# One hand-listed order replaced by another in an attention and gated-convolution kernel, with all eight weight units' low words merged on VectorE

## Chip, cores, metric

The kernel runs on one core of a Trainium2 chip. The metric is the device time of one execution in microseconds; a kernel's time is the median of several runs.

## What is computed

For 8 batches, 8 heads, 576 tokens and a head size of 64, the reference computes softmax attention inside chunks of 64 tokens, and then a gated layer on the joined heads (width 512), all in float32:

```python
scores = scale * np.matmul(q_c, k_c.transpose(0, 1, 2, 4, 3))      # chunks of 64
attn = np.exp(scores - max) ; attn = attn / (sum + 1e-9)
x = attn @ v_c                                                     # tokens x 512
gate = sigmoid(sum over k of conv_w[k] * x[s - 4 + k])             # 5 taps, causal
out = (gate * (x @ w_val)) @ w_out
```

## The kernel before

The 4608 tokens are worked on in nine groups of 512 (0 to 8). Each group has two pairs of 128 rows of the width (p = 0, 1); a pair's tile holds two halves (b = 0, 1). The last group, 8, collects the last 64 tokens of every batch and needs the last four columns of the groups before it.

Both big products are made from split operands: each operand is a high word rounded to TensorE's fp32r format and a low word with what is left, and three products (high x high, low x high, high x low) are added. The weights arrive as 64-bit numbers and are split on the chip too. A weight matrix (v for w_val, o for w_out) is split in four units, 0 to 3.

The order of all the work is written out by hand. The string `ORDER` (lines 19 to 82) lists pieces; the loop at the end of the kernel calls them one by one, and each engine runs its instructions in that order (`run`, line 136, records every instruction, so all carry line 137 in the profile). A list of slots, `SLOTS` (lines 85 to 95), says which buffer each new tile takes: SBUF tiles z, PSUM banks b, and two buffers for exponentials, e. A piece that reuses a buffer waits for its last reader.

The pieces that the text speaks of, with their arguments (g group, p pair, n weight matrix, c unit or quarter of the width):

- `lw`, `lq`, `lk`, `lv` (lines 164 to 195): loads on SP's queue; a third number loads one half, 256 KB, else 512 KB.
- `w1` to `w9`, `wa`, `wb` (lines 218 to 285): the splitting of a weight unit. `w1` clamps, `w2` scales, `w3` takes the sign, `w4` joins the bits, `w6` rounds the high word. The low 32 bits come in either by `w5` (line 249, a ScalarE multiply) and `w8` (line 258, a multiply on GpSimd, or on VectorE as `w8D`), or by `w58` (line 262, one VectorE instruction for both). Then `wa` subtracts and `wb` adds (GpSimd, or VectorE as `waD`, `wbD`), or, for units 1 to 3 of v, TensorE sums three terms (`Q`, line 273) and ScalarE copies them out (`wc`).
- `S` (line 287): scores, 32 small matmuls per half. `mx` maxima, then one of three ways to the exponential: `sb` and `ex` (lines 333, 336: VectorE subtracts the maximum, ScalarE takes the exponential of the whole tile); `mh`, `M`, `exM` (lines 342 to 359: the maximum is split in two words, eight matmuls in all subtract it in PSUM, and ScalarE reads the exponential from there); or `ng` and `ea` (lines 366, 370: ScalarE takes it row by row, with the maximum as the bias, and sums along). `sm` or `rc`: sums and reciprocals.
- `nm` (line 393; `nmD` on VectorE): normalization. `T` transposes, `ec` copies them out, `A` the weighted sums of v. `xr`, `xd` (lines 439, 444): high and low word of x; `xc`: x itself, for the taps.
- `k0`, `k`, `kx`, `kk` (lines 487 to 535): first tap and the others, kx and kk for two groups at once. `sg` sigmoid.
- `V` (line 548): product of x with w_val, three matmuls, or one of the three if a fourth number is given. `vc` copies it out, `gs` multiplies by the gate, `gr` and `gd` make high and low word.
- `P` (line 574): product with w_out, three matmuls. `oc`, `o1` copy out, `st`, `s1` store. `W` (line 603): matmuls on zeros ahead of the first data.

A letter behind a name moves the piece: D to VectorE, G to GpSimd.

Of the kernel before, what the change touches and what calls it, by code (L numbers as in the profile page):

```python
# [31 lines left out]
vc 0 1,lk 2 0,S 2 0 0,lv 1 1,S 2 0 1,mx 2 0,V 0 0 3 0,V 0 1 0 1,V 0 0 1 2,lv 3 1,sb 2 0,V 0 1 3 0,lv 2 1,k 0 2 2,w3 o 2,nm 1 1,
xc 1 0,w5 o 2,T 1 1,ec 1 1,V 1 0 0,w1G o 0,V 1 0 1,k 0 1 3,ex 2 0,sm 2 0,vc 0 0,w1G o 1,A 1 1,xr 1 1,xd 1 1,k0 1 1,w2 o 2,
w5 o 0,lk 2 1,S 2 1 0,S 2 1 1,mx 2 1,V 1 2 0,V 1 3 0,V 1 3 1,ng 2 1,V 1 1 3,k 0 2 4,xc 1 1,w4 o 2,V 1 1 0,V 1 1 2,V 1 0 2,
lq 7 1,V 1 2 2,k 0 0 3,k 0 3 4,hc 0 1,lq 4 0,w2 o 0,nm 2 0,T 2 0,V 1 2 1,k 0 2 3,k 0 0 2,w3 o 1,k 0 0 4,k0D 1 0,lk 4 0,V 1 1 1,
# [4 lines left out]
ea 3 1,nm 3 0,wa o 3,V 2 0 1,sb 4 0,wbD o 0,wbD o 3,V 2 2 1,rc 3 1,V 2 0 3,w6 o 2,gr 0 1,V 2 3 2,T 3 0,ec 3 0,lv 5 1,vc 2 1,  # L40
lq 4 1,lk 5 1,gr 0 0,V 2 0 2,V 2 1 3,vc 2 0,S 4 1 0,waD o 2,A 3 0,xc 3 0,ex 4 0,S 4 1 1,lq 8 0,nmD 3 1,gdD 0 1,P 0 2 3,P 0 3 3,
k 1 0 4,lv 8 0,wbD o 2,P 0 3 2,gdD 0 0,w4 o 1,w7 o 1,w6 o 1,w8 o 1,wa o 1,T 3 1,ec 3 1,lk 7 1,mx 4 1,P 0 2 0,xr 3 0,hc 1 0,
k0 1 2,k0 2 3,lk 6 0,P 0 3 0,P 0 2 2,P 0 0 2,sb 4 1,sm 4 0,A 3 1,P 0 0 3,wb o 1,lv 6 0,ex 4 1,hc 1 1,xd 3 0,hc 2 0,sm 4 1,
P 0 3 1,xr 3 1,xc 3 1,lq 5 1,xd 3 1,P 0 2 1,S 5 1 1,S 5 1 0,P 0 1 0,oc 0 1,mx 5 1,ng 5 1,V 3 1 0,k 1 1 2,k0 2 0,k 2 0 4,V 3 1 2,
k 1 2 1,k0 2 2,k 1 1 1,k 2 2 4,lk 6 1,nm 4 0,k 1 2 3,k 1 1 3,k0 1 3,k 2 3 2,k 1 3 1,ea 5 1,k 1 2 2,k0 2 1,P 0 1 1,V 3 1 1,T 4 0,
ec 4 0,V 3 0 0,k 1 3 3,k 1 1 4,k 1 0 2,sg 1 0,k 1 2 4,P 0 0 0,V 3 0 3,V 3 1 3,k 1 3 4,nm 4 1,T 4 1,ec 4 1,P 0 0 1,k 2 1 4,
lv 4 1,rc 5 1,V 3 2 3,V 3 3 2,k 1 3 2,k 2 1 2,V 3 3 3,V 3 3 1,V 3 3 0,lv 4 0,gs 1 0,sg 1 1,gs 1 1,gr 1 0,lq 5 0,V 3 0 1,P 0 1 3,
k 2 1 1,V 3 2 1,lk 8 0,k 2 0 2,V 3 0 2,vc 3 0,P 0 1 2,oc 0 0,V 3 2 2,V 3 2 0,gr 1 1,A 4 0,S 5 0 0,vc 3 1,k 2 3 1,S 5 0 1,xr 4 0,
gdD 1 0,P 1 3 0,P 1 2 0,xc 4 0,hc 4 0,lk 7 0,gdD 1 1,P 1 0 2,P 1 1 3,k 2 2 3,P 1 2 3,mx 5 0,xd 4 0,P 1 1 0,sb 5 0,ex 5 0,
k 2 1 3,P 1 2 1,lq 7 0,nm 5 1,T 5 1,lq 8 1,P 1 2 2,k 2 0 3,k 2 2 1,k 2 3 4,P 1 3 2,lq 6 0,P 1 3 3,k 2 0 1,k0 4 0,k 2 2 2,  # L50
P 1 3 1,k 2 3 3,P 1 0 1,sg 2 0,gs 2 0,sg 2 1,P 1 1 1,gs 2 1,ec 5 1,gr 2 0,P 1 0 0,P 1 1 2,P 1 0 3,oc 1 1,oc 1 0,S 6 0 1,gd 2 0,
lv 5 0,S 6 1 0,S 6 1 1,S 6 0 0,A 4 1,sm 5 0,nm 5 0,P 2 1 1,gr 2 1,gd 2 1,P 2 1 0,P 2 0 1,lk 8 1,P 2 0 0,mx 6 1,mx 6 0,sb 6 0,
sb 6 1,S 7 0 1,ex 6 0,sm 6 0,nm 6 0,S 7 0 0,A 5 1,xc 4 1,mx 7 0,P 2 1 3,P 2 1 2,P 2 0 3,xr 4 1,xd 4 1,lv 7 0,P 2 0 2,st 0 1,
P 2 2 2,xr 5 1,ex 6 1,sm 6 1,xd 5 1,xcD 5 1,kx 4 2,P 2 3 1,st 1 1,sb 7 0,ex 7 0,P 2 3 3,kk 4 2 3,P 2 2 1,oc 2 0,st 0 0,P 2 2 0,
T 5 0,ec 5 0,P 2 3 0,P 2 3 2,P 2 2 3,oc 2 1,sm 7 0,hc 2 1,S 7 1 1,S 7 1 0,nm 6 1,S 8 0 0,S 8 0 1,T 6 0,ec 6 0,hc 0 0,V 4 0 2,
hc 5 1,V 4 0 0,nm 7 0,mx 7 1,sb 7 1,mx 8 0,ex 7 1,T 6 1,ec 6 1,sb 8 0,ex 8 0,V 4 0 3,A 5 0,xc 5 0,lv 6 1,A 6 1,xc 6 1,S 8 1 1,
sm 7 1,nm 7 1,sm 8 0,xr 5 0,S 8 1 0,mx 8 1,V 4 1 0,V 4 0 1,xd 5 0,hc 6 1,V 4 1 3,xr 6 1,xd 6 1,sb 8 1,V 4 1 2,k0D 4 1,T 7 1,
V 4 1 1,vc 4 0,k0D 5 0,lv 8 1,T 7 0,kk 4 2 4,nm 8 0,V 4 2 2,k 4 1 3,st 1 0,ec 7 1,st 2 0,ec 7 0,kk 4 2 2,T 8 0,ec 8 0,hc 4 1,
ex 8 1,V 4 2 1,k 5 0 1,V 4 3 3,A 6 0,xc 6 0,A 7 0,xr 6 0,kk 4 2 1,sm 8 1,xd 6 0,xc 7 0,xr 7 0,A 8 0,V 4 3 1,xr 8 0,V 4 3 2,
# [641 lines left out]
```

## Time and profile before

| | us |
|---|---|
| median of 3 runs (lowest, highest) | 286.02 (285.7, 286.69) |
| the profiled execution, device time | 287.65 |
| its span, first to last instruction | 285.9 |
| TensorE matmuls busy | 273.0 |
| VectorE busy | 245.3 |
| ScalarE busy | 192.1 |
| GpSimd busy | 56.6 |

PE is TensorE (PEld its weight loads), DVE VectorE, ACT ScalarE, POOL GpSimd, SP the engine whose queue issues the loads and stores. In the names of tiles z and ys are SBUF buffers, b PSUM banks, e_row exponentials, mx maxima, rs sums. In a row of instructions the arrow points from what is read to what is written; "x64" is a count. Square brackets at a row's end hold how long the engine had been idle and whose work released it; "issue" means that the profile shows nothing it waited for. Stage and break are told by TensorE's idle time, since that engine is the busiest.

### The profile page before, as it was taken

Reading aid. Unit: us, or ns where it says so; the run is one execution under the profiler, and the core shown is the slowest. Engines: PE = TensorE matmul, PEld = TensorE weight load, DVE = VectorE, ACT = ScalarE, POOL = GpSimd, SP = SyncE. Lnnn points to the kernel's source line nnn. Section 1 sums busy time; section 2 is a strip of 40 time slices with the busy share of each in tenths; the row PEclk is TensorE's granted clock in tenths of the full one; section 3 lists DMA queues with packets and bytes.
Section 4 is the critical chain, followed back from the end, with each engine's and each line's share of the span. In section 5 each row is a group of like instructions: output and inputs, shape, how many; then the busy total and the mean of one; then the engine's idle time right before and its main releaser. Section 6 shows DMA issues by size and latency. Waiting matters only on the chain.

```text
span 285.9 us, 7884 instructions
## 1 busy us (share of the span) xinstructions
PE 273.0 (96%) x3378; PEld 219.5 (77%) x3378; DVE 245.3 (86%) x322; ACT 192.1 (67%) x345; POOL 56.6 (20%) x58
## 2 busy tenths in 40 slices
...
GB/s 212 389 408 407 404 406 409 314 230 149 220 6 14 135 221 202 97 270 255 70 150 2 5 0 5 0 0 2 0 0 1 2 0 40 34 76 147 147 302 212
DMA packets 14754, 42.46 MB, mean 149 GB/s; under 512 B 1536, under 2 KB 1792, under 8 KB 14720
## 3 DMA queue, kind: packets, MB, share of 16 engines
...
## 4 chain that ended last, share of the span: by engine, by line
PE 88%; DVE 4%; DMA 3%; issue 2%; SPq 1%; ACT 1%; DVEq 0%
PE b L137 88%; DVE z L137 3%; DMA z<-in_q 3%; SPq L137 1%; ACT z L137 1%; DVE mx L137 0%; DVE e_row L137 0%; DVEq L137 0%
## 5 line engine op out<-in xcount | busy, mean ns | idle before, releaser
L137 PE MATMUL b<-z,v_hi 128*128 128x512 f32 x288 | 96.4, 403 | 1.5 <-DVE z L137 1.4
L137 PE MATMUL b<-o_hi,z 128*128 128x512 f32 (+1 forms) x296 | 94.7, 392 | 0.0
L137 ACT COPY z<-b 128x1024 f32<-128x1024 f32 (+2 forms) x65 | 61.0, 963 | 42.4 <-PE b L137 37.5
L137 PEld LDWEIGHTS b<-z,v_hi 128*128 128x128 f32 x288 | 53.7, 188 | 16.4 <-DVE mx L137 1.9
L137 PEld LDWEIGHTS b<-o_hi,z 128*128 128x128 f32 x296 | 55.2, 188 | 12.7
L137 PE MATMUL b<-z,v_lo 128*128 128x512 f32 x144 | 56.3, 397 | 1.7 <-issue 1.7
L137 PE MATMUL b<-o_lo,z 128*128 128x512 f32 (+1 forms) x148 | 57.5, 389 | 0.0
L137 DVE SCALAR_TENSOR_TENSOR z<-z,cw,z 128x508 f32<-128x508 f32 (+3 forms) x80 | 55.8, 742 | 0.1
L137 POOL TENSOR_TENSOR z<-e_row,rs 128x1024 f32<-128x1024 f32 (+1 forms) x15 | 28.0, 1866 | 63.9 <-ACT z L137 24.7
L137 ACT ACTIVATE z<-z 128x1024 f32<-128x1024 f32 (+3 forms) x27 | 22.3, 837 | 17.6 <-DVE z L137 17.6
L137 DVE TENSOR_TENSOR z<-z,z 128x1024 f32<-128x1024 f32 (+3 forms) x25 | 30.7, 1244 | 2.3 <-ACT z L137 2.2
L137 PEld LDWEIGHTS b<-o_lo,z 128*128 128x128 f32 x148 | 28.0, 189 | 5.8
L137 DVE SCALAR_TENSOR_TENSOR ys<-ys,cw 128x1018 f32<-128x1018 f32 (+7 forms) x32 | 31.1, 1008 | 0.9 <-ACT ys L137 0.7
L137 PEld LDWEIGHTS b<-z,v_lo 128*128 128x128 f32 x144 | 27.1, 188 | 5.5
L137 PEld LDWEIGHTS b<-z,z 64*64 64x64 f32 x1088 | 19.3, 143 | 8.8 <-issue 5.4
L137 PE MATMUL b<-z,z 64*64 64x64 f32 x1088 | 21.6, 230 | 4.5 <-issue 3.5
L137 DVE TENSOR_REDUCE mx<-b 128x16 f32<-128x1024 f32 (+1 forms) x19 | 22.0, 1164 | 4.4 <-PE b L137 4.2
L137 DVE TENSOR_TENSOR z<-b,z 128x1024 fp32r<-128x1024 f32 (+1 forms) x19 | 21.9, 1156 | 3.1 <-ACT z L137 2.4
L137 ACT CAST z<-b 128x1024 fp32r<-128x1024 f32 (+1 forms) x19 | 18.4, 985 | 5.3 <-PE b L137 3.8
L137 ACT ACTIVATE e_row<-b,mx 128x64 f32<-128x64 f32 x72 | 21.4, 359 | 0.4 <-DVE mx L137 0.4
L137 ACT ACTIVATION_READ_ACCUMULATOR e_row<-b,mx 128x1 f32 x72 | 18.0, 252 | 0.0
L137 DVE TENSOR_REDUCE rs<-e_row 128x16 f32<-128x1040 f32 (+1 forms) x14 | 16.6, 1183 | 0.7 <-ACT e_row L137 0.7
...
## 6 DMA issues: line engine op xcount, KB each, us to landing
...
```

What stands on the lines that cost most here:

```text
L137: return tc.keep_in_program_order(fn(*args, **kwargs))
```

## The change

`ORDER` and `SLOTS` are replaced as a whole; no function is changed. What is computed stays the same. The new list has 1024 pieces in place of 1033:

- all eight units (v 0 to 3, o 0 to 3) use `w58`; before, v 3 alone. The seven `w5` on ScalarE, the `w8D` of v 0, 1, 2 and the `w8` of o 0 to 3 are gone;
- `wb` of o 0, 2, 3 and `wa` of o 2 go from VectorE to GpSimd;
- pair (0, 1) takes the exponential row by row in both halves (before: the first half), pair (0, 0) by `sb` and `ex` (before: `M`); `M` is not used any more;
- `k0` is on VectorE 4 times in place of 9, `kx` once in place of twice; `nm` on VectorE 4 times in place of 2; `xc` 5 1 and `o1` 8 3 go to ScalarE;
- the first loads come as v 3, taps, v 1, k, q (first half of pair (0, 1)), v 2; before, v 2 came ahead of k and q. v 0 comes ahead of group 1's q;
- every later piece has another place; TensorE's products, loads and stores are the same in number and size.

```diff
-ORDER = """lw v 3,zw,W 3,w1 v 3,w2 v 3,lc,w1 c 0,w2 c 0,zi,zs 0,W 9 22,w3 c 0,lw v 1,w3 v 3,w4 v 3,w6 v 3,zs 1,lw v 2,w7 v 3,lk 0 1 0,
-lq 0 1 0,w1 v 1,w2 v 1,lk 0 1 1,w3 v 1,w58 v 3,w4 v 1,zr 1,w3 v 2,lq 0 0 0,lq 0 1 1,Q v 3,w4 c 0,w7 c 0,w7 v 1,S 0 1 0,w5 v 1,
-lk 0 0 1,w5 c 0,w8D c 0,lk 0 0 0,w5 v 2,w1 v 2,w8D v 1,w6 v 1,Q v 1,mx 0 1 0,ng 0 1 0,lq 0 0 1,S 0 1 1,w2 v 2,w4 v 2,w7 v 2,
-wc v 3,w9,ea 0 1 0,S 0 0 0,w8D v 2,S 0 0 1,w6D v 2,Q v 2,wc v 2,mx 0 1 1,wc v 1,mh 0 1 1,M 0 1 1,exM 0 1 1,mx 0 0,mh 0 0,M 0 0,
-exM 0 0,zr 0,rc 0 1 0,nmD 0 1 0,T 0 1 0,ec 0 1 0,lq 1 0,lw v 0,w1 v 0,lk 1 0,S 1 0 1,w2 v 0,w3 v 0,sm 0 1 1,S 1 0 0,lv 0 1,
-A 0 1 0,xr 0 1 0,nm 0 1 1,T 0 1 1,V 0 3 2 0,V 0 2 2 0,xc 0 1 0,lw o 3,V 0 2 2 1,ec 0 1 1,k0 0 2,V 0 3 2 1,A 0 1 1,sm 0 0,w5 v 0,
-mx 1 0,xd 0 1 0,nm 0 0,sb 1 0,xc 0 1 1,xr 0 1 1,w3 o 3,T 0 0,w4 v 0,ec 0 0,V 0 3 2 2,V 0 0 2 1,V 0 1 2 1,lq 1 1,ex 1 0,
-V 0 0 2 0,V 0 3 3 0,V 0 3 3 1,w1G o 3,lv 0 0,A 0 0,w6 v 0,xr 0 0,V 0 1 3 1,w7 v 0,w8D v 0,wa v 0,lv 1 0,xd 0 1 1,V 0 1 3 2,
-V 0 2 3 2,V 0 0 3 2,sm 1 0,xc 0 0,lk 1 1,S 1 1 1,S 1 1 0,V 0 0 3 1,V 0 0 1 0,k0 0 3,V 0 2 1 1,V 0 2 0 1,nm 1 0,xd 0 0,V 0 2 1 0,
-V 0 2 3 1,V 0 0 0 2,w2 o 3,mx 1 1,lq 2 0,lw o 2,T 1 0,V 0 0 0 0,w5 o 3,wbD v 0,V 0 2 1 2,k0 0 0,lw o 1,w5 o 1,V 0 2 3 0,
...
-S 3 1 0,xc 2 0,w7 o 0,k 1 0 1,gs 0 0,gs 0 1,w8 o 0,A 2 1,xr 2 1,xd 2 1,w8 o 2,S 3 1 1,mx 3 1,V 2 3 1,k 1 0 3,ex 3 0,xc 2 1,
...
-o1D 8 3,s1 8 3,P 8 1 1,o1 8 2,P 8 1 2,P 8 1 3,o1 8 1,P 8 0 2 0,s1 8 1,P 8 0 3 0,s1 8 2,P 8 0 1 0,P 8 0 0 0,P 8 0 1 1,P 8 0 3 1,
-o1 8 0 0,s1 8 0 0,P 8 0 0 1,o1 8 0 1,s1 8 0 1"""
...
+ORDER = """zi,zw,lw v 3,w3 v 3,W 9 22,zs 1,w1 v 3,W 3,lc,w1 c 0,w5 c 0,w3 c 0,w2D v 3,lw v 1,w4 v 3,w7 v 3,w2 c 0,w3 v 1,lk 0 1 0,zs 0,
+w1 v 1,lq 0 1 0,lw v 2,lk 0 1 1,lq 0 1 1,w6 v 3,w4 c 0,w58 v 3,Q v 3,lq 0 0 0,lk 0 0 0,w2 v 1,w4 v 1,w6 v 1,w7 v 1,S 0 1 0,
+w58 v 1,Q v 1,w1 v 2,mx 0 1 0,w7 c 0,wc v 3,ng 0 1 0,w8D c 0,w3 v 2,w2 v 2,w4 v 2,ea 0 1 0,lk 0 0 1,S 0 1 1,mx 0 1 1,S 0 0 0,
+lq 0 0 1,S 0 0 1,lw v 0,w6 v 2,lq 1 0,w7 v 2,ng 0 1 1,w58 v 2,zr 0,zr 1,rc 0 1 0,mx 0 0,sb 0 0,ea 0 1 1,w1G v 0,Q v 2,nm 0 1 0,
+T 0 1 0,wc v 1,rc 0 1 1,lk 1 0,S 1 0 0,w3 v 0,ex 0 0,nmD 0 1 1,T 0 1 1,wc v 2,lv 0 1,sm 0 0,nm 0 0,ec 0 1 0,S 1 0 1,mx 1 0,
+w2 v 0,A 0 1 0,ec 0 1 1,xr 0 1 0,xd 0 1 0,A 0 1 1,xc 0 1 1,xc 0 1 0,T 0 0,xr 0 1 1,V 0 1 2 1,sb 1 0,ec 0 0,V 0 1 2 2,ex 1 0,
+V 0 2 3 0,V 0 3 3 1,V 0 3 2 2,xd 0 1 1,V 0 3 3 2,w4 v 0,w6 v 0,lv 0 0,A 0 0,lw o 3,lq 1 1,w3 o 3,lk 1 1,S 1 1 0,S 1 1 1,xr 0 0,
+V 0 0 3 1,V 0 2 2 0,V 0 0 0 0,V 0 1 1 0,w7 v 0,xc 0 0,V 0 3 2 0,V 0 2 1 0,w1G o 3,w2 o 3,V 0 2 2 2,w9,V 0 1 3 1,w58 v 0,wa v 0,
+V 0 3 2 1,sm 1 0,k0 0 0,V 0 2 3 1,lw o 2,xd 0 0,k0 0 2,mx 1 1,nm 1 0,V 0 2 2 1,wbD v 0,V 0 3 0 2,T 1 0,V 0 0 1 2,ng 1 1,k0 0 3,
+k 0 3 3,V 0 3 3 0,V 0 2 1 1,V 0 0 0 1,V 0 1 2 0,V 0 2 1 2,lw o 0,w1 o 0,k 0 0 2,w4 o 3,k0 0 1,V 0 2 0 2,k 0 1 2,k 0 0 1,
+V 0 2 0 1,V 0 3 1 2,w7 o 3,V 0 0 0 2,V 0 0 1 0,lw o 1,w3 o 0,ec 1 0,lv 1 0,V 0 3 1 0,V 0 2 3 2,V 0 3 0 0,V 0 0 2 1,V 0 1 1 2,
+lq 4 1,V 0 0 2 2,w58 o 3,V 0 3 0 1,V 0 1 3 2,ea 1 1,A 1 0,xr 1 0,lk 2 1,lk 2 0,w2 o 0,k 0 3 1,w3 o 1,V 0 0 1 1,rc 1 1,V 0 1 1 1,
...
+V 1 1 3,vc 1 0,nm 2 1,T 2 1,gs 0 0,k 0 2 2,wa o 0,ec 2 1,xc 2 0,V 2 1 1,V 2 0 1,k 1 0 1,w58 o 2,S 3 1 1,sg 0 1,gs 0 1,A 2 1,
+xr 2 1,xd 2 1,S 3 1 0,V 2 2 1,lv 4 0,ex 3 0,V 2 1 0,V 2 3 1,V 2 2 0,V 2 1 3,xc 2 1,V 2 3 0,lk 6 1,mx 3 1,V 2 2 3,sm 3 0,ng 3 1,
...
+P 5 0 1,V 8 1 2,k 3 1 2,gr 6 1,gs 7 1,k0D 8 0,gdD 4 1,vc 8 1,k 3 2 3,gdD 6 1,P 4 0 3,P 4 1 2,P 6 2 2,gs 6 0,k0 3 3,gr 6 0,
...
+o1 8 2,P 8 3 3,P 8 1 2,P 8 1 1,P 8 1 0,o1 8 1,st 7 0,s1 8 1,st 4 1,P 8 0 1 0,P 8 3 0,P 8 3 2,P 8 0 1 1,P 8 0 2 0,s1 8 2,o1 8 3,
+s1 8 3,P 8 0 2 1,P 8 0 3 1,P 8 0 3 0,o1 8 0 0,s1 8 0 0,P 8 0 0 1,o1 8 0 1,s1 8 0 1"""
...
```

## Rows read from the trace of the kernel before

**Rows 1.** The page, engines' busy time, share of the span and instructions.

```profile
PE 273.0 (96%) x3378; PEld 219.5 (77%) x3378; DVE 245.3 (86%) x322; ACT 192.1 (67%) x345; POOL 56.6 (20%) x58
```

**Rows 2.** The chain that ended last: start us, us, what.

```profile
22.29 8.96 PE b L137 x186
31.25 1.73 issue
...
129.33 1.80 issue
131.13 151.80 PE b L137 x1381
```

**Rows 3.** Timeline of TensorE: start us, us, instruction, idle before it.

```profile
69.42 0.72 PE L137 MATMUL b<-z,v_hi 128*128 128x512 f32 x2 [1.38 <-DVE z L137]
```

**Rows 4.** Windows: stretch, length, busy by engine, PEclk, DMA share, GB/s.

```profile
10.00:100.00 90.00, 84.75 (x1515) 67.76 (x1516) 83.69 (x126) 81.46 (x223) 32.76 (x26) 1.00 0.69 265
120.00:140.00 20.00, 18.20 (x369) 15.22 (x369) 16.36 (x18) 12.03 (x13) 10.54 (x7) 0.91 0.65 213
180.00:220.00 40.00, 40.00 (x174) 32.26 (x173) 39.91 (x49) 23.00 (x26) 0.34 (x1) 1.00 0.00 1
10.00:20.00 10.00, 8.40 (x181) 5.90 (x182) 9.59 (x25) 7.00 (x25) 0.41 (x1) 1.00 1.03 404
```

**Rows 5.** Timeline of all engines, first 25 us.

```profile
8.66 0.49 PE L137 MATMUL b<-z,signed 128*128 128x512 f32 x1 [0.67 <-DVE z L137]
...
9.98 0.69 PE L137 MATMUL b<-z,z 64*64 64x64 f32 x32 [0.82 <-DMA z<-in_q]
...
12.11 0.32 ACT L137 ACTIVATE e_row<-b,mx 128x64 f32<-128x64 f32 x1 [0.36 <-DVE mx L137]
...
13.69 1.42 PE L137 MATMUL b<-z,z 64*64 64x64 f32 x64 [0.69 <-issue]
...
14.35 0.24 ACT L137 ACTIVATION_READ_ACCUMULATOR e_row<-b,mx 128x1 f32 x1
...
23.42 0.69 PE L137 MATMUL b<-z,z 64*64 64x64 f32 x32
...
24.05 1.09 PE L137 MATMUL b<-ident,z 128*128 128x128 f32 x8
```

**Rows 6.** Groups of instructions by form: count, busy us, mean ns, idle before.

```profile
L137 DVE SCALAR_TENSOR_TENSOR z<-z,z 128x512 fp32r<-128x512 uint32 x1 | 0.7, 683 | 0.0
...
L137 DVE TENSOR_SCALAR z<-z,cw 128x512 f32<-128x512 f32 x7 | 3.3, 481 | 0.0
...
L137 DVE TENSOR_TENSOR e_row<-b,mx 128x1024 f32<-128x1024 f32 x12 | 14.7, 1222 | 0.9 <-POOL z L137 0.3
...
L137 DVE TENSOR_REDUCE rs<-e_row 128x16 f32<-128x1040 f32 x13 | 15.9, 1221 | 0.7 <-ACT e_row L137 0.7
...
L137 ACT ACTIVATE e_row<-e_row 128x1024 f32<-128x1024 f32 x12 | 12.8, 1068 | 2.6 <-DVE e_row L137 2.6
...
L137 POOL TENSOR_TENSOR z<-e_row,rs 128x1024 f32<-128x1024 f32 x14 | 27.0, 1925 | 45.8 <-ACT z L137 24.7 <-DVE rs L137 11.9 <-ACT e_row L137 9.1
```

**Rows 7.** Timelines of GpSimd and VectorE: the products with the gate.

```profile
62.99 3.96 POOL L137 TENSOR_TENSOR z<-z,z 128x512 f32<-128x512 f32 x2 [2.36 <-DVE z L137]
...
63.48 4.55 DVE L137 TENSOR_TENSOR z<-z,z 128x1024 f32<-128x1024 f32 x2
...
219.54 2.35 DVE L137 TENSOR_TENSOR ys<-z,ys 128x1024 f32<-128x1024 f32 x2
```

**Rows 8.** Timeline of TensorE: small matmuls of groups 4, 6.

```profile
123.45 1.11 PE L137 MATMUL b<-z,ys 64*64 64x64 f32 x64
...
131.13 3.17 PE L137 MATMUL b<-z,z 64*64 64x64 f32 x112 [1.80 <-issue]
```

**Rows 9.** Windows from the start to each break, columns as in rows 4.

```profile
0.00:31.30 31.30, 26.27 (x473) 17.22 (x474) 24.53 (x52) 22.12 (x51) 7.95 (x14) 1.00 0.96 358
0.00:129.35 129.35, 121.25 (x1994) 94.63 (x1995) 117.29 (x175) 110.66 (x257) 40.88 (x39) 1.00 0.68 250
```

More of the change, by code (lines that the diff above doesn't have):

```diff
@@ L32 @@
[L32 to L35, printed above, removed]
@@ L40 @@
[L40 to L43, printed above, removed]
@@ L44 @@
[L44 to L59, printed above, removed]
@@ new lines @@
+k 0 1 3,w1G o 2,w2 o 2,V 0 0 3 2,V 0 1 0 2,xc 1 0,V 0 1 0 0,w6 o 3,nm 1 1,T 1 1,ec 1 1,ex 2 0,V 0 0 3 0,sm 2 0,k0 1 0,V 1 0 0,
+V 1 1 1,lq 2 1,lv 1 1,A 1 1,S 2 1 1,xr 1 1,xd 1 1,vc 0 0,S 2 1 0,mx 2 1,V 1 1 0,k0 1 1,hc 0 1,ng 2 1,lq 6 1,lq 3 0,V 1 0 1,
+w1G o 1,w2 o 1,V 1 2 0,xc 1 1,w3 o 2,w4 o 0,w4 o 2,k 0 0 3,V 1 2 2,w7 o 2,V 1 2 3,k 0 2 4,w7 o 0,k 0 0 4,V 1 1 2,lv 2 1,V 1 0 3,
+lk 4 0,k 0 2 1,V 1 0 2,lk 3 0,lv 2 0,ea 2 1,lk 6 0,w58 o 0,rc 2 1,k 0 3 4,w6 o 0,wa o 3,V 1 2 1,k 0 1 1,lq 3 1,nm 2 0,T 2 0,
@@ new lines @@
+V 2 2 2,ea 3 1,V 2 3 2,w4 o 1,V 2 0 0,w7 o 1,T 3 0,V 2 0 2,ec 3 0,rc 3 1,nmD 3 1,k 1 0 2,w58 o 1,hc 2 0,lv 3 1,V 2 1 2,vc 2 0,
+S 4 1 1,S 4 1 0,lq 5 0,vc 2 1,lv 3 0,wb o 3,ex 4 0,A 3 0,k0D 2 2,mx 4 1,sb 4 1,xr 3 0,wa o 2,w6 o 1,P 0 2 3,wa o 1,T 3 1,
+P 0 3 3,sm 4 0,P 0 3 0,wb o 1,ec 3 1,lk 5 0,ex 4 1,P 0 2 0,sm 4 1,xc 3 0,lq 5 1,xd 3 0,A 3 1,xc 3 1,xr 3 1,xd 3 1,S 5 1 0,
+S 5 1 1,mx 5 1,k0 1 3,ng 5 1,P 0 2 1,k 1 3 3,wb o 2,P 0 3 2,lq 7 0,P 0 2 2,k0 2 0,P 0 3 1,k 1 3 2,hc 1 0,V 3 2 0,lv 5 0,V 3 1 2,
@@ new lines @@
+k 1 0 3,k0 2 1,V 3 2 2,lv 6 1,oc 0 1,V 3 2 1,V 3 0 1,V 3 2 3,k0 1 2,k 1 1 3,k 1 2 3,k 1 1 4,V 3 1 3,S 5 0 0,k 1 2 4,st 0 1,
+k 1 1 1,S 5 0 1,V 3 3 2,V 3 3 3,nm 4 0,k 1 0 4,lv 7 1,V 3 0 0,ea 5 1,T 4 0,k0 2 3,ec 4 0,k 1 1 2,V 3 1 1,k 1 3 4,V 3 0 3,rc 5 1,
+k 1 2 2,nm 4 1,V 3 3 1,k 2 0 4,k 1 2 1,lv 4 1,sg 1 0,lk 8 0,P 0 1 1,V 3 3 0,P 0 0 0,k 1 3 1,mx 5 0,sg 1 1,sb 5 0,lv 5 1,vc 3 1,
+lk 7 1,gs 1 1,gr 1 1,V 3 0 2,k 2 0 2,k 2 2 2,gdD 1 1,P 0 0 3,V 3 1 0,vc 3 0,T 4 1,ec 4 1,lq 6 0,P 0 1 2,k 2 2 3,gs 1 0,gr 1 0,
@@ new lines @@
+k 2 1 4,P 0 1 0,P 0 0 2,k 2 3 2,P 1 2 3,gdD 1 0,k 2 1 1,P 1 1 2,k 2 3 1,P 1 2 2,k 2 1 2,A 4 0,P 1 3 3,ex 5 0,xc 4 0,hc 1 1,
+k 2 3 3,P 0 1 3,P 1 3 0,P 1 3 1,k 2 0 3,P 1 3 2,P 0 0 1,xr 4 0,oc 0 0,k 2 0 1,k 2 1 3,sg 2 0,k 2 2 4,P 1 0 1,P 1 1 3,hc 3 1,
+k 2 2 1,P 1 1 0,nm 5 1,P 1 0 2,P 1 2 1,k 2 3 4,sg 2 1,T 5 1,ec 5 1,gs 2 0,gr 2 0,gd 2 0,P 1 2 0,P 1 1 1,P 1 0 3,gs 2 1,P 1 0 0,
+S 6 0 0,S 6 0 1,gr 2 1,gd 2 1,oc 1 0,xd 4 0,sm 5 0,A 4 1,oc 1 1,xr 4 1,S 6 1 1,S 6 1 0,P 2 0 1,mx 6 0,nm 5 0,lq 7 1,P 2 0 0,
@@ new lines @@
+xc 4 1,sb 6 0,ex 6 0,xd 4 1,mx 6 1,lv 8 0,P 2 1 2,P 2 0 3,P 2 1 3,sm 6 0,A 5 1,xc 5 1,nm 6 0,sb 6 1,lv 6 0,lk 7 0,S 7 0 1,
+xr 5 1,S 7 0 0,mx 7 0,ex 6 1,sb 7 0,kx 4 2,lv 8 1,P 2 0 2,xd 5 1,P 2 1 1,ex 7 0,P 2 1 0,sm 6 1,nm 6 1,oc 2 0,P 2 2 2,sm 7 0,
+P 2 2 0,T 5 0,P 2 3 3,S 7 1 1,S 7 1 0,mx 7 1,sb 7 1,lq 8 1,ec 5 0,S 8 0 0,nm 7 0,st 1 1,S 8 0 1,mx 8 0,lv 7 0,hc 4 1,P 2 3 1,
+ex 7 1,sb 8 0,st 0 0,T 6 1,ec 6 1,sm 7 1,P 2 2 3,hc 4 0,T 7 0,ec 7 0,P 2 2 1,hc 3 0,P 2 3 0,ex 8 0,kk 4 2 1,k0D 4 0,T 6 0,
```

62 lines of the change are left out of this document (31 added, 31 removed), and 12 rows, old and new, of the table z.

## The prediction

> **What bounds the kernel now.** I read the page's busy times first: TensorE is busy 96% of the span, VectorE 86%, so TensorE has only 12.9 us of the 285.9 us span to give [rows 1, 4]. The chain of waits shows where: TensorE's stream proper starts at 22.29 and then runs almost unbroken to 282.93 (131.13 + 151.80); the last copy and store take the rest [rows 2]. Breaks inside are 1.73 us at 31.25, 1.38 us before 69.42 that VectorE releases, and 1.80 us at 129.33 [rows 2, 3]. So the total is: the wait for the stream, plus TensorE's work, plus three breaks, plus a tail of 3 us. A new order can move the start and the breaks, and no more.
>
> The windows tell which engine could take TensorE's place. Of the 90 us from 10 to 100 VectorE works 83.7 and idles 6.3; from 180 to 220 it idles 0.1 of 40, while TensorE never waits [rows 4]. ScalarE and GpSimd are far from full [rows 1].
>
> **The change part by part.** *TensorE.* Its matmuls stay, but for the eight that subtract the first pair's maxima. They lie ahead of 22.29, so they are counted in the start below and not again.
>
> *Merged low words.* Seven units change from a ScalarE multiply and a separate VectorE or GpSimd multiply to one VectorE instruction of 0.68 us, 4.8 us in all [rows 6]. Off VectorE go three separate multiplies, and three additions and a subtraction handed to GpSimd: seven of the same size, about as much again. Five first taps of 0.48 us and one of double length go to ScalarE (some 3 us off VectorE); two normalizations and a subtraction of 1.22 come on (3.7), one copy of a pair, half a copy and half a sum go (2.4). The rest is small steps. Net some 2 us less of VectorE's 245 [rows 1, 6]. ScalarE keeps most of its 94 us of idle, GpSimd of its 229 [rows 1]. No total shifts the bound; where the work stands does.
>
> *The start.* In the new list the third weight unit is loaded behind the first q and k. Its 512 KB take 1.3 us at the 404 GB/s of that stretch [rows 4], so the first scores, which began at 9.98 after 0.82 us of waiting [rows 5], could begin 1.3 earlier; but TensorE first ends the first unit's low-word sum (8.66 + 0.49) [rows 5], so they gain 0.8. The loads ahead of the other pair's scores are the same ones in both lists, so these still end about 14.4, as the unsplit burst does (half of 1.42 from 13.69) [rows 5]. From there the path runs: 0.45 behind a small VectorE step, maxima 1.15, subtraction 1.15 (1.22 less the overlap seen between neighbours), 0.3 behind the second row-by-row block on ScalarE (eight rows take 12.11 to 14.59 [rows 5], two blocks end about 17.0, a copy of a low word follows), exponential 1.05, 0.1, sum and reciprocal 1.45, normalization on GpSimd 1.9, transposes 1.05 [rows 5, 6]. 14.4 + 8.6 = 23.0: then the stream begins, 0.7 later than at 22.29. But two bursts that stood inside the stream, 0.69 and 1.09 us, are already done by then [rows 5]: 1.8 - 0.7, about **1.0 us gained**. Bounds: +1.0 (each of ten hand-offs 0.2 late) to -2.0 (the stream's first pieces, which need only the early half, slip in front). The load of the last weight unit moves ahead of the next group's q on SP's queue, 1.3 us for whoever is behind; those scores are due at about 17.7 and run behind a transpose, not on the path. On GpSimd this unit's clamp stands ahead of the first normalization and waits for the load (about 15.0); this holds back transposes that end by 19.4, well before 22.
>
> *The middle.* The 1.38 us break [rows 3] follows two VectorE products that took 4.55 us where the same pair takes 2.35 later; GpSimd ran two separate low-word multiplies beside them, 3.96 us [rows 7]. These multiplies are gone, and one subtraction stands near one of the products now: half of the 2.2 us comes back. Against that the new list is tighter: adding durations of these forms [rows 6] along both lists, up to each first use of a low word of x or of the gated product, TensorE's listed work exceeds VectorE's by 0.5 us at the least before, and falls 1.6 short after. These 2.1 us are lost if VectorE idles as much as before. I take it that it does not: from 10 to 31 my list of the new start leaves VectorE without work for about 0.5 us. So most of the break goes: **-0.9**, between -1.4 and +2.1.
>
> *Late stage.* The same sums give at least 2.9 us before, and 0.0, 0.1 and 0.5 at the first products with the low words of groups 5, 6 and 4 after. VectorE is full there [rows 4]; **+0.3**, between 0 and +1.5. Behind a late low word stand all later output products, since TensorE works in list order.
>
> *The break at 129.* It is 1.80 us, and then 112 small matmuls take 3.17 us where 64 take 1.11 [rows 8], so 1.2 more: the granted clock is 0.91 over that stretch [rows 4], which is part of it at the lower level (1.2 GHz) after the idle. Nothing in the trace releases this break, nor the one at 31.25. I keep both: 0, between -3.0 and +3.0, as a rival. They come after 473 and 1994 matmuls [rows 9], each with a weight load. The Trainium skill (Runtime: NRT & Kernel Launch, Instruction fetch mechanics) says that instructions come in blocks of 256 and that crossing a block's edge is mostly hidden: 946 and 3988 instructions, with waits on top, would be near 1024 and 4096, edges that stay where they are in a list of the same work. If crossings are hidden as that page has it, the breaks belong to the old order and go; the sum would then be 281.4, not 284.4.
>
> *The tail.* Last product, copy, small store: as before. One 512 KB store is put off to among the last small ones; the queue has a product's time for it: 0, at most +0.5.
>
> Sum: -1.0 - 0.9 + 0.3 = **-1.6 us**. The profiled execution took 287.65 us, 285.9 of it span, 1.6 above the median of 286.02; the difference is carried to the median: **284.4**.
>
> **The rivals.** *VectorE becomes the bound* (slower): with the idle of 6.3 us kept, the 2.1 us are lost in the middle, and about 1.0 late, and the start's gain holds: 286.02 - 1.0 + 2.1 + 1.0 = 288.1. It decides where VectorE idles over about 4 us of 10 to 100. For it: full windows [rows 4], the thinner margins. Against: total work falls by 2, and the early idle that the new list fills. Chance 0.22.
> *The unreleased breaks go with the order*: -3.0 more, 281.4. For it: nothing shown holds them; against: they can be tied to the number of instructions. Chance 0.12. The other way about, one more such break: 287.4, chance 0.06.
> *The gains cancel*: the row-by-row blocks hold ScalarE so long that the first exponential of the other half is 1 us later than I have it, and the 0.9 stays: about 286. Chance 0.20.
> The forecast has 0.40.
>
> **How the numbers follow.** A measurement here can tell about 0.3% (0.9 us) from no change. Faster: 0.40 + 0.12 = 0.52; same 0.20; slower 0.22 + 0.06 = 0.28. The range, 281.5 to 288.0, reaches to the rivals on both sides; the likeliest case alone has 282.6 to 285.5.
>
> **What would show it.** In the changed profile: the first value product near 23.0, with both of the first pair's weighted sums ahead of it; VectorE idle from 10 to 100 under 5 us; no TensorE idle of 1 us released by VectorE from 55 to 75; breaks without a releaser still near 470 and 1990 matmuls. VectorE as the releaser of over 2 us of TensorE's idle, or a first value product after 24.5, would prove it wrong.

## The result: 2.4 us faster, by another way than forecast

The changed kernel takes 283.3 us (median of 5 runs, 282.83 to 283.99) where the kernel before, run beside it, takes 285.7 (285.12 to 286.69): a ratio of 0.9913, 95% interval 0.9886 to 0.994. The forecast was 284.4, faster by 1.6. The gain has the right sign and is 0.8 us larger than forecast. But of the four terms of the sum none came out as written: the start and the middle gave nothing, the late loss did not come, and the gain stands where the sum had a zero, at the breaks that nothing releases.

The page of the changed kernel, engines' busy time as in [rows 1]:

```profile
PE 270.6 (96%) x3370; PEld 217.5 (77%) x3370; DVE 241.9 (86%) x306; ACT 195.0 (69%) x359; POOL 54.0 (19%) x56
```

Its chain that ended last, as in [rows 2] (start us, us, what):

```profile
25.92 5.85 PE b L136 x147
31.76 0.16 issue
...
60.86 84.16 PE b L136 x1424
145.02 0.26 issue
145.28 132.93 PE b L136 x996
```

TensorE's work is 2.4 us shorter, VectorE's 3.4. The profiled execution took 283.3 us (span 281.4), that of before 287.65 (span 285.9): 4.5 us of span, of which 2.4 are TensorE's busy time and the rest its idle time. Before's profiled execution took longer than any of the five runs beside it, so this comparison overstates. Of the 2.4 us, about 1.3 are one burst of 112 small matmuls that ran slowly in that execution (3.17 us [rows 8], 1.86 in run 1 below); the eight matmuls that subtracted the first pair's maxima (1.47 us in run 1) are gone too, but they lay ahead of the first value product and belong to the start. In the chain the two breaks of 1.73 and 1.80 us [rows 2] have shrunk to 0.16 and to nothing; at the same number of matmuls (1993) TensorE now runs on. A new break of 0.26 is at 145.

The waits of TensorE, summed (engine, what it waited for, us in total, times, longest), in a second profiled execution of the kernel before (the first run below, span 284.5):

```profile
PE b L138 <- issue: 4.7, 6, 1.9
PE b L138 <- DVE z L138: 1.6, 2, 1.4
PE b L138 <- DVE warm L138: 1.2, 1, 1.2
PE b L138 <- DMA z<-in_q: 0.8, 1, 0.8
```

The same view of the changed kernel:

```profile
PE b L136 <- DVE z L136: 2.2, 2, 1.7
PE b L136 <- POOL o_lo L136: 1.5, 1, 1.5
PE b L136 <- DVE warm L136: 1.2, 1, 1.2
PE b L136 <- ACT e_row L136: 1.1, 1, 1.1
PE b L136 <- POOL z L136: 0.5, 1, 0.5
PE b L136 <- issue: 0.4, 2, 0.3
```

This is the result in one view. "Issue", time for which the profile knows no releaser, falls from 4.7 us to 0.4 (it is 5.3 in the first profile of before). Waits for the other engines grow, from 3.6 us of these rows to 6.5. The timeline of TensorE shows where (start us, us, instruction, idle before it):

```profile
9.47 0.51 PE L136 MATMUL b<-z,signed 128*128 128x512 f32 x1 [1.74 <-DVE z L136]
...
24.22 0.48 PE L136 MATMUL b<-z,v_lo 128*128 128x512 f32 x1
...
60.86 1.06 PE L136 MATMUL b<-ident,z 128*128 128x128 f32 x8 [1.50 <-POOL o_lo L136]
```

And the windows, to be read against [rows 4]:

```profile
10.00:100.00 90.00, 85.80 (x1570) 68.60 (x1571) 87.16 (x132) 83.23 (x236) 32.74 (x27) 0.98 0.79 295
120.00:140.00 20.00, 20.00 (x513) 16.83 (x512) 19.06 (x21) 15.20 (x16) 12.74 (x9) 1.00 0.31 91
10.00:20.00 10.00, 8.38 (x173) 5.54 (x174) 9.29 (x23) 9.01 (x39) 1.65 (x2) 0.83 1.04 404
```

VectorE idles 2.8 us from 10 to 100 (6.3 before). From 120 to 140 TensorE is busy all the time (18.2 before), at the full clock, and the DMA engines carry 91 GB/s where they carried 213. From 10 to 20 the granted clock is 0.83, part of it at the lower of the two levels, 1.2 GHz, behind the idle of 1.74 us before 9.47.

### The profile page after: what moved, and what is told of

Same layout as the page of the kernel before. It is cut to its first block, busy times and chain, and to the rows that moved or that the text cites. A ratio compares the mean times of both kernels' runs of the same rounds, so it can differ in the third digit from the quotient of the medians.

```text
span 281.4 us, 7853 instructions
## 1 busy us (share of the span) xinstructions
PE 270.6 (96%) x3370; PEld 217.5 (77%) x3370; DVE 241.9 (86%) x306; ACT 195.0 (69%) x359; POOL 54.0 (19%) x56
## 4 chain that ended last, share of the span: by engine, by line
PE 82%; DVE 6%; ACT 4%; issue 3%; DMA 2%; POOL 2%; SPq 0%; POOLq 0%; ACTq 0%
PE b L136 82%; DVE z L136 3%; DMA z<-in_moe_w_val 2%; ACT z L136 2%; ACT e_row L136 2%; DVE mx L136 1%; POOL z L136 1%; DVE e_row L136 1%; DVE rs L136 1%; POOL o_lo L136 0%; SPq L136 0%; DVE cw_h L136 0%; POOLq L136 0%; ACTq L136 0%
## 5 line engine op out<-in xcount | busy, mean ns | idle before, releaser
L136 PE MATMUL b<-o_hi,z 128*128 128x512 f32 (+1 forms) x296 | 96.3, 393 | 0.0
L136 DVE SCALAR_TENSOR_TENSOR z<-z,cw,z 128x508 f32<-128x508 f32 (+3 forms) x80 | 59.1, 776 | 0.3
L136 DVE TENSOR_TENSOR z<-z,z 128x1024 f32<-128x1024 f32 (+1 forms) x22 | 26.7, 1222 | 12.2 <-ACT z L136 12.2
L136 POOL TENSOR_TENSOR z<-e_row,rs 128x1024 f32<-128x1024 f32 (+1 forms) x13 | 24.2, 1861 | 43.7 <-DVE rs L136 15.2
L136 DVE SCALAR_TENSOR_TENSOR ys<-ys,cw 128x1022 f32<-128x1022 f32 (+3 forms) x24 | 29.9, 1273 | 0.0
L136 ACT ACTIVATE e_row<-b,mx 128x64 f32<-128x64 f32 x80 | 23.8, 358 | 0.5 <-DVE mx L136 0.3
L136 ACT ACTIVATE z<-z 128x1024 f32<-128x1024 f32 (+1 forms) x19 | 17.1, 913 | 7.9 <-DVE z L136 7.9
L136 PE MATMUL b<-ident,z 128*128 128x128 f32 x128 | 17.1, 274 | 3.8 <-POOL o_lo L136 1.5
L136 ACT ACTIVATION_READ_ACCUMULATOR e_row<-b,mx 128x1 f32 x80 | 20.0, 252 | 0.0
L136 PEld LDWEIGHTS b<-ident,z 128*128 128x128 f32 x128 | 14.6, 140 | 6.4 <-POOL z L136 2.2
```

What stands on the lines that cost most here:

```text
L136: return tc.keep_in_program_order(fn(*args, **kwargs))
```

## The experiments

No run leaves out any of the work. Pieces are those of the order list. Times with a ratio to the kernel before are medians of 6 to 11 runs; the others are one run with its profile, and single runs of the kernel before, 40 of them beside the twelve experiments, lie between 284.4 and 288.9 us.

**1. The kernel before once more.** No edit.

> The kernel before once more, for its breaks that nothing releases. If they belong to the program (its order or its place in the stream of instructions), TensorE shows again 1.7 us of idle near 31 us and 1.8 us near 129 us, with the slower small matmuls behind it, and the span is near 285.9 us. If they belong to the one execution, at least the later one is gone and the span is near 283 us.

Measured: 286.3 us (span 284.5; the kernel before had a median of 285.3 in the runs beside it). Its two long breaks come back at the places of [rows 2] (timeline of TensorE):

```profile
33.11 0.39 PE L138 MATMUL b<-z,v_lo 128*128 128x512 f32 x1 [1.86 <-issue]
...
131.29 1.86 PE L138 MATMUL b<-z,z 64*64 64x64 f32 x112 [1.54 <-issue]
```

So they belong to the program and not to one execution. The slow burst behind the second one does not: 112 small matmuls take 1.86 us here at a granted clock of 1.00, and took 3.17 in the first profile [rows 8].

**2 to 7. The same lists with 64, 128 and 192 more instructions ahead of them.** The tiny warming matmuls near 2 us are 32, 64 or 96 more (each is two instructions, a weight load and a matmul); everything behind keeps its order. With 64 more the last number is 86, with 96 more 118.

```diff
-W 9 22
+W 9 54
```

> The kernel before with 32 more small matmuls on zeros ahead of the first data, so 64 more instructions in TensorE's stream, and nothing else. If the breaks sit at fixed places of the stream, the first long one comes again after about 473 matmuls in all, 32 products or transposes earlier in the work than before. If they belong to a place of the work, it stands ahead of the same product, after about 505 matmuls. Time within 1 us of the kernel before either way.

> The changed kernel with 32 more tiny matmuls (64 instructions on TensorE's stream) in its warming burst near 2 us, about 0.5 us of work in time in which TensorE waits anyway. Theory A (the breaks that nothing releases come where an edge of a 256-instruction block falls into or just behind a burst of small matmuls; the new list won because its edges happen to fall well): edges move by 64 instructions, breaks of 1 to 5 us without a releaser appear at matmul numbers that had none, idle put down to issue grows from 0.4 us to over 4 us, and the time is 288 to 297 us, as the kernel before went from 285.3 to 296.6 under the same edit. Theory B (the new order itself keeps them away): idle put down to issue stays under 1 us, time 283 to 284.

> The kernel before with 64 more tiny matmuls (128 instructions) in the same warming burst. Theory A (edges of instruction blocks): a third set of breaks, at places other than 33, 47 and 131 us of the unshifted list and other than 25, 67, 132, 159 and 173 us of the list shifted by 64; time between 286 and 298, span longer by the idle put down to issue. Theory B (the extra matmuls themselves cost, at the start): the same breaks as unshifted and the stream's start later by 1 us, 286 to 288.

> The changed kernel with 64 more tiny matmuls (128 instructions) in its warming burst; the pair to the kernel before under the same edit, which took 296.2 us. Theory A (where block edges fall decides, and the unshifted order was lucky): idle put down to issue from 3 to 10 us, time 287 to 296. Theory B (the new order has fewer places at which an edge costs): under 3 us of such idle, and at least 4 us faster than the kernel before under the same edit, 284 to 290. The longer warming burst can delay the first low-word sum by up to 0.5 us in both.

> The changed kernel with 96 more tiny matmuls (192 instructions) in its warming burst: the fourth of four evenly spaced positions of the block edges. Theory A (luck of the unshifted position): idle put down to issue from 3 to 10 us, 287 to 297. Theory B (fewer costly places in the new order): 284 to 290, faster than the kernel before under the same edit. Up to 1 us of delay at the start comes from the longer warming burst.

> The kernel before with 96 more tiny matmuls (192 instructions) in its warming burst. By theory A its time lies between 286 and 297 and may be under that of the changed kernel with the same edit; by theory B it lies above it by 2 us or more. Up to 1 us of delay at the start comes from the longer warming burst.

Measured: time of the profiled run and TensorE's idle put down to issue in it (us; the first line is run 1 and the changed kernel's own profile):

| instructions added | before: time | issue | new order: time | issue | time gained | issue gained |
|---|---|---|---|---|---|---|
| 0 | 286.3 | 4.7 | 283.3 | 0.4 | 3.0 | 4.3 |
| 64 | 296.6 | 11.1 | 288.4 | 2.7 | 8.2 | 8.4 |
| 128 | 296.2 | 10.7 | 293.2 | 9.3 | 3.0 | 1.4 |
| 192 | 286.3 | 3.4 | 284.4 | 0.9 | 1.8 | 2.5 |

Sixty-four instructions that are nowhere near the critical path cost the kernel before 11 us, where the expectation had under 1. The matmuls themselves are not what costs: the warming burst lasts 6.22 us with 34 of them in run 1, and as long with 66 (timeline of TensorE, kernel before with 64 more):

```profile
1.19 6.22 PE L138 MATMUL b<-warm 128*128 128x512 bf16 x66 [1.19 <-DVE warm L138]
```

The new order is ahead in all four lines, so theory B holds in part; but it is not free of breaks (9.3 us in the third line), so theory A holds as well, and of the four positions the one that both kernels have by chance is the new order's best. With one run at each position, how much of its lead is the order and how much the choice of positions stays open.

Take the issue time off each time: 281.6, 285.5, 285.5, 282.9 before and 282.9, 285.7, 283.9, 283.5 in the new order, means of 283.9 and 284.0. Apart from these breaks the two orders are equal on the mean, though single lines differ by 1.3 against the new order to 1.6 for it. The breaks cost more than their idle time: the granted clock of the whole span is 1.00, 0.98, 0.99, 1.00 before and 0.99, 0.99, 0.99, 1.00 in the new order, and in the second line before, TensorE is busy 277.2 us in place of 272.7. That part is still in the times after the subtraction.

Where do the larger breaks fall? The windows from the start to the end of a break count the matmuls up to it (in brackets, first TensorE, then its weight loads). The kernel before with 64 more:

```profile
0.00:25.09 25.09, 19.40 (x347) 12.21 (x347) 19.28 (x45) 15.28 (x40) 4.39 (x11) 1.00 0.93 349
0.00:132.35 132.35, 120.42 (x1995) 94.64 (x1996) 116.08 (x174) 110.75 (x256) 37.66 (x37) 0.98 0.68 248
0.00:159.52 159.52, 146.36 (x2502) 115.97 (x2503) 136.12 (x195) 126.06 (x272) 50.11 (x48) 0.97 0.61 223
0.00:172.87 172.87, 158.17 (x2755) 126.09 (x2756) 148.77 (x209) 135.15 (x282) 52.93 (x50) 0.97 0.57 206
```

The kernel before with 128 more:

```profile
0.00:24.83 24.83, 18.20 (x347) 11.72 (x347) 18.28 (x43) 13.60 (x37) 3.76 (x10) 1.00 0.94 347
0.00:53.71 53.71, 45.90 (x854) 33.79 (x855) 41.88 (x79) 40.36 (x101) 13.60 (x19) 0.97 0.98 374
0.00:134.35 134.35, 119.72 (x1995) 94.15 (x1996) 116.40 (x174) 110.94 (x256) 37.89 (x37) 0.99 0.67 244
```

The new order with 128 more:

```profile
0.00:24.64 24.64, 18.59 (x346) 11.69 (x346) 18.11 (x39) 14.69 (x50) 4.40 (x11) 1.00 0.94 355
0.00:33.73 33.73, 23.45 (x472) 15.43 (x472) 22.20 (x47) 21.08 (x59) 8.86 (x15) 1.00 0.96 369
```

With 473 and 1994 of the unshifted kernel [rows 9], each of these lies at about 346, 473, 854, 1994, 2502 or 2755 matmuls, whatever the order and the shift. These numbers are multiples of some 127 apart (127, 3 times 127, 9 times 126.7, 4 times 127, 2 times 126.5). One break put down to issue is of another kind: 0.7 us before 14.01 in run 1 comes after 106 matmuls, and with 64 instructions more after 138, ahead of the same scores, so it stays with its work. It is in the first two lines of the table, before; without it the means are 284.2 and 284.0. The table of DMA queues in the page of the changed kernel says what comes as often as the other breaks:

```profile
q8 instruction: 26, 0.43, 0.6%
```

26 packets of instructions, 16 KB each; from one edge to the next TensorE runs some 127 matmuls and as many weight loads, 253 instructions. The times of the packets in the traces fit edge by edge. In the nine profiles (the first of before and the eight of the table) 36 breaks of over 0.1 us without a releaser lie at such a count; counted from the edge at 219 matmuls, the n-th edge belongs to the n-th packet, and in all 36 TensorE goes on 1.2 to 1.6 us after that packet has landed. At no edge, with or without a break, does it go on sooner. So TensorE's stream comes in blocks, the edges are at fixed counts, a break at one is a block that came late, and an added instruction moves not the edges but the work that stands there. The clearest case is the edge at 1994. In the kernel before with 64 more it costs 4.67 us (timeline of TensorE):

```profile
132.36 0.48 PE L138 MATMUL b<-z,ys 64*64 64x64 f32 x3 [4.67 <-issue]
```

In the changed kernel, whose count is 1993 at 128.33, the same edge lies inside this burst of its timeline, whose 64 matmuls run without a break:

```profile
128.03 1.16 PE L136 MATMUL b<-z,z 64*64 64x64 f32 x64
```

**What makes a block late, read from the traces and not tried by itself.** Around the edge at 1994 the kernel before (run 1) starts its instruction packet late: from 124.0 to 128.9 the queue table shows data packets alone, from 128.9 to 130.0 it has this row (one packet of 0.02 MB, 5.2% of 16 engines' 1.1 us, so 0.9 us), and TensorE goes on at 131.29:

```profile
q8 instruction: 1, 0.02, 5.2%
```

The previous edge was one step of 127 matmuls earlier, near 124.8. In between the DMA engines are full, 327 GB/s at a share of 0.97 (window of run 1):

```profile
124.80:129.00 4.20, 4.20 (x122) 3.62 (x112) 3.73 (x4) 3.19 (x4) 3.46 (x3) 1.00 0.97 327
```

They work on two loads and three stores of 512 KB that SyncE had issued just before (timeline of its queue, run 1):

```profile
121.83 0.33 SPq L138 DMA_DIRECT2D z<-in_k  x1
122.20 0.42 SPq L138 DMA_DIRECT2D z<-in_v  x1
122.68 2.95 SPq L138 DMA_DIRECT2D out<-z  x3
```

In the changed kernel SyncE issues one load between 112 and 134 (timeline of its queue):

```profile
120.14 0.33 SPq L136 DMA_DIRECT2D z<-in_v  x1
```

Its packet comes between 123.5 and 125, and around it the DMA engines carry next to nothing (windows):

```profile
122.90:124.00 1.10, 1.10 (x89) 1.10 (x85) 1.00 (x2) 1.05 (x2) 1.10 (x2) 1.00 0.10 22
124.00:128.00 4.00, 4.00 (x43) 3.01 (x35) 3.51 (x4) 3.82 (x4) 3.48 (x2) 1.00 0.00 0
```

This reads as an instruction fetch that stands in line behind data. Over the nine profiles, packets that start after TensorE has passed the previous edge do so a median of 3.5 us behind it where the DMA engines were at a share of 0.9 or more in between (78 packets), and 0.8 us where they were under 0.1 (68). But some of the latter start 5 us late too, up to 5.7, so full DMA engines are not all that delays a start. The reading would also say why most breaks lie ahead of 70 us and near 130, where transfers are dense, and why none over 0.3 us comes after 173: there a block of long products lasts some 29 us, and any fetch is in time. Full DMA engines are not needed: the breaks of 1.24 and 1.54 us at 159 and 173 (kernel before, 64 more) come with the DMA engines at a share of 0.01, behind bursts of small matmuls that use up a block in a few us. No run moved a transfer alone, so that the block comes late is shown, and how much of this is the queue and how much the short block stays open.

**8. The first unit's merged low word earlier.** It is put ahead of the second unit's clamp, which waits for a load.

```diff
-... w3 v 1,lk 0 1 0,zs 0, ... w4 c 0,w58 v 3,Q v 3
+... w58 v 3,w3 v 1,lk 0 1 0,zs 0, ... w4 c 0,Q v 3
```

> The new order with the merged low word of unit v 3 ahead of the next unit's sign and clamp, for which VectorE waits 1.43 us for the load. If TensorE's 1.74 us of idle before 9.47 us and the half clock after it set the start, the low-word sum ends near 7.8 us, the stretch from 10 to 20 us is at full clock, the first value product comes 0.6 to 1.0 us before 24.2 us and the time falls by 0.6 to 1.0 us, to about 282.5. If the later ScalarE rows set the start, less than 0.3 us.

Measured: 283.41 us, ratio to the kernel before 0.9931 (0.9916 to 0.9947). The wait of 1.74 us at 9.47 goes and the low-word sums of the first two units start 0.7 and 1.5 us earlier, but then the scores wait for their loads (0.66 at 12.69, 0.64 at 14.02, 0.98 at 19.01). The first value product comes at 23.90 for 24.22, and the break at 145 grows from 0.26 to 0.73. The time does not change: the wait is real and costs nothing here, since the loads are next in line.

**9. Two taps away from GpSimd's normalization.** In the changed kernel the break before 60.86 is a transpose that waits for a bank which VectorE's subtraction of maxima frees. (The profile names GpSimd's `o_lo`, which ends at the same time, near 60.7; this run decides between the two.) VectorE's timeline of that stretch:

```profile
52.98 1.41 DVE L136 SCALAR_TENSOR_TENSOR z<-z,cw,z 128x508 f32<-128x508 f32 x2
...
55.28 2.96 DVE L136 SCALAR_TENSOR_TENSOR z<-z,cw,z 128x508 f32<-128x508 f32 x2
...
59.49 1.23 DVE L136 TENSOR_TENSOR e_row<-b,mx 128x1024 f32<-128x1024 f32 x1
```

GpSimd's timeline of the same stretch:

```profile
55.50 2.20 POOL L136 TENSOR_TENSOR z<-e_row,rs 128x1024 f32<-128x1024 f32 x1 [6.23 <-ACT o_hi L136]
```

Two taps take 2.96 us beside a normalization that takes 2.20 (1.9 in [rows 6]); the same pair at 52.98, while GpSimd is idle, takes 1.41.

```diff
-... rc 2 1,k 0 3 4, ... k 0 1 1, ... sb 3 0 ...
+... k 0 1 1,rc 2 1, ... sb 3 0,k 0 3 4, ...
```

> The new order with two taps of group 0 moved: one ahead of the reciprocal of pair (2, 1), one behind the subtraction of pair (3, 0). If TensorE's 1.50 us of idle before 60.86 us comes from VectorE's two taps running beside GpSimd's normalization (2.96 us for the pair where 1.41 is usual), which hold up the subtraction that frees the bank, the idle falls under 0.5 us and the time by about 1 us, to 282.3. If GpSimd's queue itself holds the transpose, nothing changes.

Measured: 283.75 us, ratio 0.9949 (0.9931 to 0.9967). The break of 1.50 goes, and the subtraction starts 2.5 us earlier (VectorE's timeline below, 56.97 for 59.49). The transposes start at 58.87, before `o_lo` ends at 60.68, so it was the subtraction that they waited for (timelines of TensorE and GpSimd):

```profile
58.87 1.04 PE L137 MATMUL b<-ident,z 128*128 128x128 f32 x8
...
59.07 1.61 POOL L137 TENSOR_TENSOR o_lo<-z,z 128x512 fp32r<-128x512 f32 x1
```

But a merged low word behind it takes 1.78 us for 0.68, two new VectorE waits of 0.22 and 0.44 come, and the break at 145 grows to 0.53. Ahead by 1.4 us at 63, it is ahead by 0.2 behind 145. VectorE's timeline:

```profile
56.97 1.23 DVE L137 TENSOR_TENSOR e_row<-b,mx 128x1024 f32<-128x1024 f32 x1
...
63.73 1.78 DVE L137 SCALAR_TENSOR_TENSOR z<-z,z 128x512 f32<-128x512 uint32 x1
```

**10. Both moves together.**

> The changed kernel with both moves that took a VectorE wait away when each was made alone: the first unit's merged low word ahead of the second unit's clamp, and the two taps out from beside GpSimd's normalization. If the two gains add and are kept: 282.0 to 282.8. If, as with each alone, what is won by 63 us is given back at the next VectorE step and at the instruction edge near 145 us: 283.0 to 283.8, no difference from the changed kernel.

Measured: 283.07 us, ratio 0.992 (0.989 to 0.9951), 11 runs: not to be told from the changed kernel (0.9913). The second case of the expectation.

**11. Seven merged low words taken apart again**, at the same places of the new list.

```diff
-w58 v 1
+w5 v 1,w8D v 1
...
-w58 o 3
+w5 o 3,w8 o 3
```

> The changed kernel with seven of its eight merged low words (all but the first unit's) back as a ScalarE multiply and a separate multiply at the same place of the list, on VectorE for the v units and on GpSimd for the o units. The count of TensorE's instructions is unchanged. The prediction's reason (separate multiplies on GpSimd slow the VectorE products beside them): the break near 61 us that VectorE's late step causes grows from 1.5 to 2.4 us or another of about 1 us appears between 45 and 75, VectorE's idle over 10 to 100 stays near 3 us; time 284.2 to 284.8. Rival (merging is worth nothing by itself: it gives VectorE as much work as the separate multiplies that are handed to GpSimd took from it, and what the pair costs is moved about): 283.0 to 283.8, with VectorE some 2.7 us less busy and GpSimd some 7 us more.

Measured: 302.18 us, ratio 1.0594 (1.0572 to 1.0617). Neither reason of the expectation: it is 19 us slower than the changed kernel. Of the 17.6 us between the spans (299.0 for 281.4) 4.7 are longer TensorE work, at a granted clock of 0.977, and some 13 are waits: 8.1 us for GpSimd and 7.5 for VectorE, where the changed kernel has 2.0 and 2.2. Only the largest break is followed here. TensorE's timeline:

```profile
64.90 1.33 PE L137 MATMUL b<-ident,z 128*128 128x128 f32 x5 [7.17 <-POOL z L137]
```

ScalarE's, the first of 16 row-by-row exponentials and the step behind the last:

```profile
54.27 0.33 ACT L137 ACTIVATE e_row<-b,mx 128x64 f32<-128x64 f32 x1
...
58.90 0.78 ACT L137 ACTIVATE z<-z 128x512 f32<-128x512 uint32 x1
```

GpSimd's:

```profile
59.76 1.55 POOL L137 TENSOR_TENSOR z<-z,z 128x512 f32<-128x512 f32 x1 [13.21 <-ACT z L137]
...
62.95 3.75 POOL L137 TENSOR_TENSOR z<-e_row,rs 128x1024 f32<-128x1024 f32 x2
```

The ScalarE half of the low word stands in the list behind these exponentials (54.27 to 58.9); GpSimd, which works in list order too, waits 13.21 us for it with two normalizations queued behind, and TensorE waits for these. Merging, then, does more than exchange VectorE work: at this place it takes a step off the way from ScalarE over GpSimd to TensorE, and the new list is laid out for that. What separate steps at places of their own would cost was not tried.

**12. The first pair row by row, in the order of before.** Eight matmuls go, eight tiny ones are added in the warming burst, so that the edges stay.

```diff
-mh 0 1 1,M 0 1 1,exM 0 1 1,mx 0 0,mh 0 0,M 0 0,exM 0 0, ... sm 0 1 1
+ng 0 1 1,ea 0 1 1,mx 0 0,sb 0 0,ex 0 0, ... rc 0 1 1
...
-W 9 22
+W 9 30
```

> The kernel before with the first pair's exponentials as in the change: no matmuls that subtract the maxima, the early half row by row on ScalarE, the late half by a VectorE subtraction and one exponential. Eight matmuls go, and eight tiny ones are put into the warming burst, so that all later instruction edges stay where they are. The prediction's reason (the first pair done this way is ready earlier): the transposes of the first weights come 0.5 to 1 us earlier than in the kernel before, 284.4 to 285. Rival (the row-by-row blocks hold ScalarE and the subtraction holds VectorE in the stretch in which both are full, as in the changed kernel, whose first value product came 1.9 us later than that of the kernel before): the first value product 0.5 to 2 us later, and the time 285.3 to 287.

Measured: 287.07 us, ratio 1.0065 (1.0047 to 1.0082), 1.6 us slower. The rival of the expectation holds: VectorE's subtraction (1.22 us, at 16.64) comes ahead of the normalization (at 18.29) that the first transposes need, and the first value product starts at 23.67, for 22.29 in the first profile of before and 21.86 in run 1. TensorE's timeline:

```profile
19.12 1.09 PE L138 MATMUL b<-ident,z 128*128 128x128 f32 x4 [2.27 <-DVE z L138]
...
23.67 0.50 PE L138 MATMUL b<-z,v_hi 128*128 128x512 f32 x1 [0.17 <-ACT z L138]
```

## Why the prediction was right in the sign and wrong in its steps

**The start, -1.0: wrong, about 0.** The step that failed is "14.4 + 8.6 = 23.0". The first value product came at 24.22, 1.9 us later than before (2.4 later than in run 1), with 1.8 us more work done by then. Two hand-offs of the start went otherwise. TensorE waits 1.74 us before 9.47, where a low word stands on VectorE behind the next unit's clamp, which waits for its load (I had walked the path of the pair, not that of the first unit's low-word sum). Only a part of that is lost: the low-word sum comes 0.8 us later than in the first profile of before and 0.4 later than in run 1, and in run 9, with the same list up to there, TensorE idles 0.52 us before 9.26. And it waits 1.1 us before 18.12, behind the second row-by-row block on ScalarE. Runs 8 and 12 say that neither was a matter of a single wait: without the first, the loads hold the scores; and the first pair done this way costs the old order 1.6 us. The bound of +1.0 ("each of ten hand-offs 0.2 late") was the right end to lean to.

**The middle, -0.9: wrong, 0.** The break of 1.38 us [rows 3] went from its place, and another of 1.50 came at 60.86, by the same mechanism: a VectorE product beside GpSimd work takes twice its time, 2.96 for 1.41 in place of 4.55 for 2.35 [rows 7]. The forecast took away the neighbour at the old place and did not look for the next place at which GpSimd and VectorE meet. Run 9 shows the price (the break goes) and the worth (nothing by 145). That VectorE's idle would shrink below 5 us was right: 2.8.

**Late, +0.3: 0.** TensorE has no wait for VectorE behind 61 us. The tail is as before, 3.2 us for 3.0.

**The breaks, kept at 0: wrong, and the gain.** Issue time fell by 4.3 us between profiled runs of 286.3 and 283.3 us. One microsecond of this lay ahead of the first value product and belongs to the start; behind it issue time fell from 3.8 to 0.4 us, and the two spans differ by 3.1. This is the rival "the unreleased breaks go with the order", with a chance of 0.12, priced at -3.0. That price was too small by the prediction's own rows: breaks of 1.73 and 1.80 and 1.2 for the slow burst are 4.7. The argument against it was "they can be tied to the number of instructions". They are: runs 2 to 7 show them at fixed counts in both orders. The error lay in what follows from that. A fixed count fixes where an edge is, and not what it costs; the order decides which work and which transfers stand around it. The Trainium skill (Runtime: NRT & Kernel Launch, Instruction fetch mechanics) has the block of 256 instructions, which agrees with the 253 matmuls and weight loads from edge to edge here. That crossing an edge is mostly hidden, as it also says, does not hold for these kernels, where edges cost 0.4 to 10.7 us in all.

**VectorE becomes the bound (0.22): no.** With 2.8 us of idle its condition of over 4 us was not met.

**The signs.** Of those named beforehand, the first value product near 23.0, no break of 1 us from 55 to 75, and breaks left near 470 and 1990 matmuls were all missed (0.16 us is left near 470). One of the two that "would prove it wrong" came true: VectorE is the releaser of 2.2 us of TensorE's idle, and of 1.5 more by run 9, where the limit was 2. That the total came out near is luck: a zero that should have been -3 to -4 stands against gains of 1.9 us that did not come.
